# A gate loop before a mixture of experts: one small copy changes its queue, and the values are loaded a turn earlier into one more buffer

## The chip, the cores and the metric

The kernel runs on one core of one Trainium2 chip. The metric is the device time of one execution in microseconds (us); it is 389.04 us before the change, the median of three executions (388.29 to 390.93).

The core has five engines that run side by side, each through its own list of instructions in order: TensorE (PE in the profile; PEld are its weight loads), VectorE (DVE), ScalarE (ACT), GpSimd (POOL) and SyncE (SP). Transfers (DMAs) are issued by SP and by POOL here. Whoever issues a transfer first waits for what it depends on, and what stands behind it in the same list waits as well.

## The reference, cut to what matters

There are two parts. The first is a linear recurrence with a complex decay for each of 4 batches and 8 heads, over 768 steps with 48 channels; its output y is the input of the second part, a mixture of experts.

```python
def _attn_ref(q, k, v, a_re, a_im):
    mag = np.sqrt(a_re * a_re + a_im * a_im)
    scale = np.minimum(mag, 0.999) / (mag + 1e-06)
    a_re_n, a_im_n = (a_re * scale, a_im * scale)
    for t in range(S):
        new_re = ar * S_re - ai * S_im          # ar, ai: step t of a_re_n, a_im_n
        new_im = ar * S_im + ai * S_re
        kv = np.einsum('bhd,bhe->bhde', k[:, :, t], v[:, :, t])
        S_re, S_im = (new_re + kv, new_im)
        y[:, :, t] = np.einsum('bhd,bhde->bhe', q[:, :, t], S_re)

def _moe_ref(x, modality_id, w_gate, modality_bias, w1, w2):
    # each of the 3072 rows goes to the one expert (of 8) that its logits name:
    # out = gate weight * (relu(x @ w1[e]) @ w2[e])
```

All inputs and the output are float32.

## The kernel before

The steps are cut into 6 chunks of 128. A chunk of one batch is a unit of work; there are 24 units, in the order of chunk and then batch, and two units of the same chunk make a group. The products of decays inside a chunk become sums of logarithms and of angles, so the recurrence turns into masked matrix products inside a chunk and one state that goes from chunk to chunk. The state is multiplied by the moduli of the whole chunk, `mt`.

A turn `w` of the main loop takes a different stage of each of several units, so that all engines have work. This is the loop, cut to the calls that matter here:

```python
for w in range(-4, NU + 1):
    even = w % 2 == 0
    x = w // 2                      # group
    n = w + 1 if w < 0 else w       # unit
    unit(values, n + 2)             # SP: load V
    if even:
        phase(load_a, x + 6)        # SP: load a_re, a_im of a group (4 DMAs)
        phase(carries, x + 4)       # SP: load the angles carried over (cb)
        phase(decays2, x + 1)       # second half of mt
        phase(fractions, x + 3)
    else:
        phase(load_qk, x + 3)       # SP: load q, k of a group (4 DMAs)
        phase(decays, x + 2)        # SP: load mt
        hats(n + 3)
    unit(turned, n + 2)             # PE: transposes tKT, tQT
    ...
    unit(inner, n + 1)              # PE: wp, up; DVE: W, mid, U, state
    ...                             # even: sums and moduli of group x + 2
    unit(outer, n)                  # PE: yp
    ...
    unit(rows, n - 1)               # PE: xw; ACT: xr; POOL: x_rows
    ...
    if casts and (w > 9 or w % 3 == 1 and w > 0):
        cast = casts.pop(0)()       # POOL: 768 KB of expert weights to bf16, DRAM to DRAM
```

The scheduler may move a few calls of a turn against each other; the order of the calls is by and large the order in which a queue issues them.

V has four buffers of its own, used in turn. Elements 48 to 63 of each row stay zero:

```python
Vs = [un.tile([L, H, 64], F32, name=f"V{i}", bufs=1) for i in range(4)]
for V in Vs:
    nc.gpsimd.memset(V[:, :, D:64], 0.0)

def values(g, b):
    V = Vs[(g * B + b) % 4]
    nc.sync.dma_start(out=V[:, :, 0:D], in_=at(v, g, b))
```

Two products read V: `up` in the stage `inner` (line 300), which makes what the chunk adds to the state, and `yp` in the stage `outer` (line 322), a turn later. With that the buffer is free again.

The moduli go through DRAM, because they are needed with channels on partitions and are made with time on partitions. `moduli` writes the last row of `pm` to `m_scr` from POOL; `decays` reads it back as `mt` from SP, on 48 partitions; `decays2` copies `mt` to the next 48 partitions, because the real and the imaginary half of the state lie below each other:

```python
def moduli(x):
    ...
    nc.gpsimd.dma_start(out=m_scr[n0:n0 + NG]..., in_=pm[L - 1:L, 0]...)    # line 225

def decays(x):
    mt = un.tile([C, NG, H], F32, name="mt", bufs=4)
    nc.sync.dma_start(out=mt[0:D], in_=m_scr[n0:n0 + NG].rearrange("i h d -> d i h"))   # line 234

def decays2(x):
    mt = box["mt", x]
    nc.sync.dma_start(out=mt[D:C], in_=mt[0:D])                             # line 241
```

The copy of line 241 can be issued only when the load of line 234 has landed. DVE then uses both halves:

```python
nc.vector.tensor_tensor(new[:], U[:], box["mt", ...][...].broadcast_to([C, H, D]), Alu.mult)   # line 310
```

Other loads on the same SP queue are `ab` (a_re and a_im, two buffers), `qk` (q and k, two buffers), `cb`, and the writes of the gate weights `gw` into `x_rows`. Other transfers on the POOL queue are `f_scr` (angles), `m_scr`, `x_rows` (the rows y for the experts, from `xr`, two buffers) and the 16 weight casts. The second part, the experts, follows the loop and isn't touched by the change.

Of the kernel before, what the change touches and what calls it, by code (L numbers as in the profile page):

```python
# [11 lines left out]
F32 = mybir.dt.float32  # L12
# [11 lines left out]
def gate_loop(nc, ctx, tc, cpool, ident, q, k, v, a_re, a_im, sel, lg, x_rows, casts, make_router):  # L24
# [4 lines left out]
    B, H, S, D = q.shape  # L29
    L = 128  # L30
    G = S // L
    J = H // 2
    C = 2 * D
# [5 lines left out]
    un = ctx.enter_context(tc.tile_pool(name="un", bufs=2))  # L39
# [26 lines left out]
    def bank(shape, name):  # L66

        full = ps.tile([128, 512], F32, name=name, tag="bank", bufs=7)
        n = 1
        for s in shape[1:]:  # L70
            n *= s
        flat = full[0:shape[0], 0:n]
        if len(shape) == 2:
            return flat
        names = " ".join(f"x{i}" for i in range(len(shape) - 1))
        return flat.rearrange(f"p ({names}) -> p {names}", **{f"x{i}": s for i, s in enumerate(shape[1:])})


    Vs = [un.tile([L, H, 64], F32, name=f"V{i}", bufs=1) for i in range(4)]
    for V in Vs:  # L80
        nc.gpsimd.memset(V[:, :, D:64], 0.0)

# [8 lines left out]
    def table(name):  # L91
        then(nc.scalar.preload_act_table_set(name))  # L92
# [8 lines left out]
    def at(x, g, b):  # L101
        return x[b, :, g * L:(g + 1) * L, :].rearrange("h t d -> t h d")
# [134 lines left out]
    def decays2(x):  # L237

        if ("mt", x) in box:
            mt = box["mt", x]  # L240
            nc.sync.dma_start(out=mt[D:C], in_=mt[0:D])

    def both(x):
        return x[:, :, None, :].broadcast_to([L, H, 2, D])
# [1 line left out]
    def hats(w):  # L246

        if not 0 <= w < NU or (hats, w) in done:
            return
        done.add((hats, w))  # L250
        x, i = w // NG, w % NG
        cs = box["cs", x]
        pm = box["pm", x]
        qk = box["qk", x]
        qp = un.tile([L, H, D], F32, name="qp")
        nc.vector.tensor_tensor(qp[:], qk[:, 0, i], pm[:, 0, i], Alu.mult)
        kp = un.tile([L, H, D], F32, name="kp")
        nc.vector.tensor_tensor(kp[:], qk[:, 1, i], pm[:, 1, i], Alu.mult)
        Kh = un.tile([L, H, 2, D], F32, name="Kh", bufs=5)
        nc.vector.tensor_tensor(Kh[:], cs[:, i], both(kp[:]), Alu.mult)  # L260
        Qh = un.tile([L, H, 2, D], F32, name="Qh", bufs=3)
        nc.vector.tensor_tensor(Qh[:], cs[:, i], both(qp[:]), Alu.mult)
        box["hats", order[w]] = Qh, Kh

    def values(g, b):
        V = Vs[(g * B + b) % 4]
        nc.sync.dma_start(out=V[:, :, 0:D], in_=at(v, g, b))

    def turned(g, b):
# [14 lines left out]
    def inner(g, b):  # L284


        Kh, KT, QT = box.pop(("turned", g, b))
        V = Vs[(g * B + b) % 4]
        W = un.tile([L, H, L // 2], F32, name="W")
        wp = bank([L, H, L // 2], "wp")  # L290
        for h in range(H):
            for s in halves:
                nc.tensor.matmul(wp[s, h, :], KT[:, h, s], QT[:, h, s], start=True, stop=True)  # L293
        nc.vector.tensor_tensor(W[:], wp, mask2[:, None, :].broadcast_to([L, H, L // 2]), Alu.mult)
        old = state.get(b)
        more = g < G - 1
        ups = [bank([C, H, D], "up") for s in halves[:1 + more]]
        for h in range(H):
            for s, up in zip(halves, ups):
                nc.tensor.matmul(up[:, h, :], Kh[s, h].rearrange("t c d -> t (c d)"), V[s, h, 0:D], start=True, stop=True)  # L300
        mid = un.tile([C, H, D], F32, name="mid", bufs=3)
        if g:
            nc.vector.tensor_tensor(mid[:], old[:], ups[0], Alu.add)
        else:
            nc.vector.tensor_copy(mid[:], ups[0])
        if more:
            U = un.tile([C, H, D], F32, name="U")
            nc.vector.tensor_tensor(U[:], mid[:], ups[1], Alu.add)
            new = un.tile([C, H, D], F32, name=f"state{b}", bufs=2)
            nc.vector.tensor_tensor(new[:], U[:], box["mt", (g * B + b) // NG][:, b % NG, :, None].broadcast_to([C, H, D]), Alu.mult)  # L310
            state[b] = new
        box["inner", g, b] = QT, W, (old, mid)

    def outer(g, b):

        QT, W, states = box.pop(("inner", g, b))
        V = Vs[(g * B + b) % 4]
        yps = [bank([128, J, L // 2], "yp") for s in halves]
        for j in range(J):
            for u in range(2):  # L320
                for s, yp, S in zip(halves, yps, states):
                    nc.tensor.matmul(yp[u * 64:(u + 1) * 64, j, :], V[s, 2 * j + u, :], W[s, 2 * j + u, :], start=j == 0, stop=S is None and j == J - 1)  # L322
        yT = un.tile([128, J, L], F32, name="yT")
        for s, yp, S in zip(halves, yps, states):
            if S is not None:
                for j in range(J):
                    for u in range(2):
                        nc.tensor.matmul(yp[u * 64:u * 64 + D, j, :], S[:, 2 * j + u, :], QT[:, 2 * j + u, s], start=False, stop=j == J - 1)  # L328
            nc.scalar.copy(yT[:, :, s], yp)  # L329
        box["outer", g, b] = yT  # L330
# [22 lines left out]
    def phase(f, x):  # L353

        if 0 <= x < NX and (f, x) not in done:
            done.add((f, x))
            f(x)

    def unit(stage, w):
        if 0 <= w < NU and (stage, w) not in done:  # L360
            done.add((stage, w))
            stage(*order[w])
# [26 lines left out]
    for w in range(-4, NU + 1):  # L389


        even = w % 2 == 0
        x = w // 2

        n = w + 1 if w < 0 else w
        unit(values, n + 2)
        if even:
            phase(load_a, x + 6)
            phase(carries, x + 4)
            phase(decays2, x + 1)  # L400
            phase(fractions, x + 3)
        else:
            phase(load_qk, x + 3)
            phase(decays, x + 2)
            hats(n + 3)
            if w == -3:
                hats(0)
        unit(turned, n + 2)
        if even:
            if x + 2 < NX:  # L410
                table(EXP)
            if w < 0:
                phase(sums, x + 2)
                phase(moduli, x + 2)
            phase(logs, x + 4)
        elif x + 3 < NX:
            table(TRIG)
            phase(arctans, x + 4)
        unit(inner, n + 1)
        if even:  # L420
            phase(sums, x + 2)
            phase(moduli, x + 2)
            for f in late:
                f(act)
            late.clear()
        unit(outer, n)
        if even:
            hats(n + 3)
            phase(tangents, x + 4)
        else:  # L430
            phase(waves, x + 3)
            phase(squares, x + 5)
        unit(rows, n - 1)
        if not even:
            phase(angles, x + 4)
        if w == 0:
            rt = make_router(ctx, ps, bank)
        marks.append(chain[-1])
        if casts and (w > 9 or w % 3 == 1 and w > 0):
            cast = casts.pop(0)()  # L440
            tc.add_manual_dep(cast.ins, marks[-3].ins.name, mybir.DependencyInfo(mybir.DependencyClass.Sync, mybir.DependencyReason.DATA), reason="spreads the casts over the turns")
        open_ = [t for t in open_ if next(t, True) is None]
        if w - 1 in takes:
            open_.append(rt.take(takes[w - 1], w, late))
            next(open_[-1])
# [337 lines left out]
def kernel(  # L783
# [37 lines left out]
    with ExitStack() as gstack:  # L821
        rt = gate_loop(nc, gstack, tc, cpool, ident, q, k, v, a_re, a_im, sel, lg, x_rows, casts, lambda where, ps, bank: Router(nc, where, tc, cpool, ps, bank, lg, x_rows, moe_modality_id, moe_modality_bias, N, Dt, E, B, S // 128))
# [31 lines left out]
```

## Time and profile before

| | before |
|---|---|
| time, median of 3 | 389.04 us (388.29 to 390.93) |
| span of the profiled execution | 385.6 us |
| PE, DVE, ACT, POOL busy | 82%, 66%, 62%, 27% |
| first part (gate loop and router) | 0 to about 280 us of the span |
| experts | about 280 us to the end |
| V loads | 24, 192 KB each, median 4.0 us from issue to landing |
| `mt` load, `mt` copy | 10 each, 3 KB, median 3.5 and 2.4 us |
| weight casts | 16, 768 KB, median 8.4 and 8.7 us |

The page's first part gives the busy share of each engine over the whole span, its second the same in 40 slices of 9.6 us, with the clock that TensorE was granted and the share of the 16 DMA engines. Both stages have different limits, so the shares over the whole span say little; what matters is where in the slices the busiest engine of a stage has a hole, and which wait ended last there. That is in the list of waits, in the timeline of an engine, and in the chain of work that ended last.

### The profile page before, as it was taken

What the parts mean: (1) busy time and instruction counts of PE and PEld (TensorE: products, weight loads), DVE (VectorE), ACT (ScalarE), POOL (GpSimd) and SP (SyncE); (2) the same over time, 40 slices, a digit from 0 to 9 for tenths busy, and PEclk for the clock granted to TensorE, in tenths of its full rate; (3) what the DMA queues carried; (4) which work ended last, traced back from release to release, by engine and by line L of the source; (5) the groups of instructions that cost most, each with busy time, mean ns of one, the idle gap of its engine ahead of it and who ended that gap; (6) DMA issues with size and microseconds to landing.
All of it is one profiled execution on the core that took longest, in us unless ns stands there. A gap on an engine that the chain in (4) does not pass through costs nothing.

```text
span 385.6 us, 11163 instructions
## 1 busy us (share of the span) xinstructions
PE 317.4 (82%) x4533; PEld 259.5 (67%) x4533; DVE 256.3 (66%) x560; ACT 239.4 (62%) x410; POOL 105.2 (27%) x149
## 2 busy tenths in 40 slices
PE   0075799999999999990899999999219999999991
PEld 0033587787888878880778898998006777777780
DVE  2559989999988999947369899334803444444340
ACT  2869999999999997974359884343022323333331
POOL 6011102121120121211012213000074776767332
PEclk9998969999999999996599999999657999999998
DMA  9998878999988899999599998930199999999961
GB/s 143 187 161 166 174 115 155 182 190 172 196 158 166 178 161 183 151 200 167 91 190 165 188 188 150 201 65 23 31 393 363 415 403 405 411 406 406 414 256 41
DMA packets 164564, 81.04 MB, mean 210 GB/s; under 512 B 143807, under 2 KB 153332, under 8 KB 164514
## 3 DMA queue, kind: packets, MB, share of 16 engines
q1 hardware_dynamic: 147922, 57.94, 62.2%
q0 software_dynamic: 16592, 22.40, 27.7%
q8 instruction: 35, 0.57, 0.6%
q14 instruction: 15, 0.12, 0.1%
HBM read 85.71 MB, written 21.11 MB: 277 GB/s over the span
## 4 chain that ended last, share of the span: by engine, by line
PE 47%; ACT 14%; DMA 10%; issue 9%; DVE 6%; SPq 6%; POOL 5%; POOLq 1%; DVEq 0%; ACTq 0%
PE h_ps L740 7%; PE up L300 6%; PE y_ps L751 6%; PE wp L293 4%; PE xw L337 4%; PE yp L328 4%; DMA V<-in_v_dram 4%; ACT sq L95 3%; PE tKT L277 3%; PE tQT L277 3%; POOL out_dram L759 3%; SPq L109 3%; PE u L161 2%; PE yp L322 2%; PE ls L211 2%
## 5 line engine op out<-in xcount | busy, mean ns | idle before, releaser
L300 PE MATMUL up<-V,Kh 64*96 64x48 f32 x704 | 40.0, 253 | 11.4 <-DMA V<-in_v_dram 11.1
L744 ACT ACTIVATE hT<-h_ps 128x512 bf16<-128x512 f32 x31 | 18.5, 597 | 45.3 <-PE h_ps L740 45.3
L300 PEld LDWEIGHTS up<-V,Kh 64*96 64x96 f32 x704 | 36.7, 167 | 13.4 <-issue 11.2
L740 PE MATMUL h_ps<-xgT,w1t 128*128 128x256 bf16 (+1 forms) x456 | 45.7, 258 | 0.0
L751 PE MATMUL y_ps<-w2t,hT 128*128 128x384 bf16 x248 | 43.5, 326 | 0.2 <-DVE hT L742 0.2
L740 PEld LDWEIGHTS <-w1t 128*128 128x128 bf16 x456 | 38.9, 100 | 5.8
L161 PE MATMUL u<-tan,turn 128*128 128x384 f32 x48 | 23.3, 571 | 22.9 <-ACT tan L95 22.9
L759 POOL DMA_INDIRECT out_dram<-y_sb,idx x31 | 31.2, 1007 | 29.7 <-ACT y_sb L755 20.0
L717 POOL DMA_INDIRECT xg<-x_rows,idx x31 | 29.9, 965 | 34.0 <-ACT idx L701 25.1
L277 PE MATMUL tKT<-ident,Kh 128*96 128x128 f32 x192 | 26.9, 285 | 8.0 <-DVE Kh L260 8.0
L751 PEld LDWEIGHTS <-hT 128*128 128x128 bf16 x248 | 23.4, 98 | 14.1 <-DVE hT L742 0.3
L92 ACT ACT_TABLE_LOAD x25 | 32.1, 1283 | 1.2 <-PEq L838 0.8
L742 DVE TENSOR_SCALAR hT<-h_ps 128x512 bf16<-128x512 f32 x31 | 21.4, 691 | 16.7 <-PE h_ps L740 11.6
L277 PEld LDWEIGHTS tKT<-ident,Kh 128*96 128x96 f32 x192 | 22.4, 133 | 11.2 <-DVE Kh L260 5.3
L329 ACT COPY yT<-yp 128x256 f32<-128x256 f32 x48 | 16.8, 376 | 19.9 <-PE yp L328 19.7
L293 PE MATMUL wp<-QT,KT 96*64 96x64 f32 x768 | 28.5, 229 | 0.0
L293 PEld LDWEIGHTS wp<-QT,KT 96*64 96x64 f32 x768 | 25.1, 141 | 4.6 <-issue 2.1
L161 PEld LDWEIGHTS u<-tan,turn 128*128 128x128 f32 x48 | 9.5, 224 | 27.5 <-issue 25.6
L337 PE MATMUL xw<-sel,yT 128*128 128x104 f32 x192 | 28.0, 291 | 0.0
L278 ACT COPY KT<-tKT 96x512 f32<-96x512 f32 x48 | 26.0, 594 | 2.3 <-PE tKT L277 2.2
L278 ACT COPY QT<-tQT 96x512 f32<-96x512 f32 x48 | 26.4, 609 | 0.5 <-PE tQT L277 0.5
L344 POOL DMA_DIRECT2D x_rows<-xr x20 | 12.4, 621 | 52.0 <-ACT xr L340 51.9
(144 smaller groups left out, 674.6 us busy)
## 6 DMA issues: line engine op xcount, KB each, us to landing
w1t<-w1b SPq DMA_DIRECT2D x19, 768.0 KB, 11.6
w2t<-w2b SPq DMA_DIRECT2D x19, 768.0 KB, 12.5
w1b<-in_moe_w_dram POOLq DMA_DIRECT2D x8, 768.0 KB, 8.4
w2b<-in_moe_w_dram POOLq DMA_DIRECT2D x8, 768.0 KB, 8.7
ab<-in_a_re_dram SPq DMA_DIRECT2D x24, 192.0 KB, 4.6
ab<-in_a_im_dram SPq DMA_DIRECT2D x24, 192.0 KB, 4.7
qk<-in_q_dram SPq DMA_DIRECT2D x24, 192.0 KB, 4.6
qk<-in_k_dram SPq DMA_DIRECT2D x24, 192.0 KB, 4.7
```

The costliest lines, as they stand in the source:

```text
L92: then(nc.scalar.preload_act_table_set(name))
L161: nc.tensor.matmul(u, turn[:], tan[:, i], start=True, stop=False)
L277: nc.tensor.transpose(tp[:, i, :], src[:, h4 + i].rearrange("t c d -> t (c d)"), ident[:])
L278: nc.scalar.copy(T[name][:, h4:h4 + 4], tp)
L293: nc.tensor.matmul(wp[s, h, :], KT[:, h, s], QT[:, h, s], start=True, stop=True)
L300: nc.tensor.matmul(up[:, h, :], Kh[s, h].rearrange("t c d -> t (c d)"), V[s, h, 0:D], start=True, stop=True)
L337: nc.tensor.matmul(xw[:, j, :], yT[:, j, :], sel[:, j, :], start=True, stop=True)
L717: nc.gpsimd.indirect_dma_start(out=xg[:], out_offset=None, in_=x_rows, in_offset=bass.IndirectOffsetOnAxis(ap=idx[:, s, 0:1], axis=0))
L740: nc.tensor.matmul(h_ps[:, f, :], w1t[:, k, ff * 128:(ff + 1) * 128], xgT[:, k, :], start=(k == 0), stop=(k == KD - 1))
L742: nc.vector.tensor_relu(hT[:, g * nf:(g + 1) * nf], h_ps[:])
L751: nc.tensor.matmul(y_ps[:], hT[:, f, s * 128:(s + 1) * 128], w2t[:, f, :], start=(f == 0), stop=(f == NF - 1))
L759: sc = nc.gpsimd.indirect_dma_start(out=out, out_offset=bass.IndirectOffsetOnAxis(ap=idx[:, s, 1:2], axis=0), in_=y_sb[:], in_offset=None, ...
```

## The change

Two things are changed, both in what SP has to issue in the gate loop. The copy of `mt` is issued from POOL, so that SP doesn't stand at it until the load of `mt` has landed. And V is loaded one turn further ahead: at turn n the load of unit n + 3 instead of n + 2, for which there is a fifth buffer. (The old call stays in the loop; every unit is loaded once, so it acts only where the new call hasn't come before it.)

```diff
-    Vs = [un.tile([L, H, 64], F32, name=f"V{i}", bufs=1) for i in range(4)]
+    Vs = [un.tile([L, H, 64], F32, name=f"V{i}", bufs=1) for i in range(5)]
@@ decays2
-            nc.sync.dma_start(out=mt[D:C], in_=mt[0:D])
+            nc.gpsimd.dma_start(out=mt[D:C], in_=mt[0:D])
@@ values, inner, outer (the same edit in each)
-        V = Vs[(g * B + b) % 4]
+        V = Vs[(g * B + b) % 5]
@@ main loop
         unit(values, n + 2)
+        unit(values, n + 3)
         if even:
```

The arithmetic and the bytes moved are the same.

More of the change, by code (lines that the diff above doesn't have):

```diff
@@ L287, in inner @@
         Kh, KT, QT = box.pop(("turned", g, b))
-        V = Vs[(g * B + b) % 4]
+        V = Vs[(g * B + b) % 5]
         W = un.tile([L, H, L // 2], F32, name="W")
@@ L316, in outer @@
         QT, W, states = box.pop(("inner", g, b))
-        V = Vs[(g * B + b) % 4]
+        V = Vs[(g * B + b) % 5]
         yps = [bank([128, J, L // 2], "yp") for s in halves]
```

## The prediction

> **What bounds the kernel now.** I read the page's 40 slices first. PE is at 8 or 9 tenths through the gate loop, except in slices 18 and 19 (173 to 193 us), where it drops to 2 tenths and its granted clock halves. The later dip, slices 27 to 29, is the router's end and isn't touched.
>
> ```profile
> PE   0075799999999999990899999999219999999991
> ...
> PEclk9998969999999999996599999999657999999998
> DMA  9998878999988899999599998930199999999961
> ```
>
> The list of waits, longest first, says what ended it: one single wait of PE for a load of V. Beside it DVE waited 6.7 us for a load of `ab` in the same stretch.
>
> ```profile
> PE up L300 <- DMA V<-in_v_dram: 11.1, 1, 11.1
> ...
> DVE tan L125 <- DMA ab<-in_a_im_dram: 7.6, 3, 6.7
> ```
>
> The table by stretches of 8.7 us (one turn) has after each stretch PE, weight loads, DVE, ACT, POOL, then granted clock, DMA share, GB/s. PE does nothing in 175.5 to 184.2 and then runs at clock 0.50. DMA is full in the hole (1.08), but had slack before it (0.63) and after it (0.53).
>
> ```profile
> 149.40:158.10 8.70, 8.67 (x201) 8.01 (x202) 8.47 (x28) 8.70 (x17) 1.99 (x3) 1.00 0.63 130
> ...
> 175.50:184.20 8.70, 0.00 (x0) 0.00 (x0) 6.75 (x12) 4.55 (x7) 0.57 (x1) 0.61 1.08 161
> 184.20:192.90 8.70, 8.01 (x105) 7.55 (x106) 3.88 (x7) 3.08 (x5) 0.00 (x0) 0.50 0.53 92
> ```
>
> What it costs: in PE's timeline the same step, the first transposes of a turn, starts at 170.77 and next at 195.03. That is 24.26 us for one turn; the chain has its neighbours at 195.19, 204.05 and 212.76, so 8.7 to 8.9 us a turn. The hole costs about 15.5 us: 11.1 of waiting, and 4.4 because the work from 184.90 to 195.03 (10.1 us) takes 5.8 two turns earlier, from 155.75 to 161.51.
>
> ```profile
> 170.77 1.04 PE L277 MATMUL tKT<-ident,Kh 128*96 128x128 f32 x8
> ...
> 195.03 1.04 PE L277 MATMUL tKT<-ident,Kh 128*96 128x128 f32 x8
> ```
>
> Why were V and `ab` late? SP's own waits lead with the line that the change moves, and SP's timeline shows where it hurt: the load of `mt` is issued at 146.18, its copy at 154.48, and everything behind the copy stands for 7.6 us. Four `ab` loads end at 170.51 (+4.5 us to landing = 175.0, when DVE resumed). The V load of turn 14 is issued at 174.09, 0.3 us after PE had finished the `wp` products before it, and lands at 184.8.
>
> ```profile
> SPq L241 <- DMA mt<-m_scr: 29.0, 10, 7.6
> ```
>
> ```profile
> 146.18 0.62 SPq L234 DMA_DIRECT2D mt<-m_scr  x1
> 154.48 0.51 SPq L241 DMA_DIRECT2D mt<-mt  x1
> 155.09 0.54 SPq L267 DMA_DIRECT2D V<-in_v_dram  x1
> ...
> 164.94 5.53 SPq L109 DMA_DIRECT2D ab<-in_a_re_dram  x1
> 170.51 1.12 SPq L110 DMA_DIRECT2D ab<-in_a_im_dram  x1
> ...
> 174.09 0.38 SPq L267 DMA_DIRECT2D V<-in_v_dram  x1
> 174.56 10.54 SPq L576 DMA_DIRECT2D x_rows<-gw  x8
> ```
>
> Why did 192 KB take 10.7 us, against a median of 4.0? Because POOL issued a weight cast (768 KB) at 173.57. The queues' shares while the cast of 162.82 ran show it: q0 (POOL's) holds the engines, q1 (SP's loads) has 5.5%.
>
> ```profile
> q0 software_dynamic: 255, 0.52, 101.3%
> q1 hardware_dynamic: 117, 0.02, 5.5%
> ```
>
> **What the Trainium skill says.** (1) "DMA: Bandwidth & Descriptors", section "Queues, rings and completion order": a DMA engine takes turns between its queues packet by packet. The lines above agree: 255 packets of 2 KB against 117 of mostly 192 bytes, so the small ones get next to no bytes. A load issued within about 8 us of a cast is late. (2) Same page, "Two DMAs through the same engine are not ordered": who reads what an earlier DMA wrote must wait for its semaphore on the issuing engine. So line 241 stands in SP until `mt` has landed; the trace agrees, 29.0 us in 10 waits. (3) Same page, "Issuing engines are not separate DMA queues": another issuer brings no more bandwidth, only issue time. I agree as to bandwidth; the trace's gain is not the 0.51 us of issuing but the 7.6 us of standing. (4) "TensorE: Matmul & The Clock Gate", "What's actually happening": after an idle window of about 3.4 us the clock halves. The trace agrees: 0.50 after a hole of 11.1 us.
>
> **The change, part by part.** *Copy to POOL.* Ten copies of 3 KB leave SP; with them go up to 29.0 us of standing and 10 × 0.5 us of issuing, nearly all hidden today. On the path is the 7.6 us before 154.48. The built program keeps each queue's order, and SP's transfers each wait for the eighth before it. If all after 146.8 moves up by 7.6, the last `ab` lands at 175.0 − 7.6 = 167.4. *V a turn earlier.* Load n+3 at turn n into the fifth buffer waits for the same release as load n+2 did with four (turn n−2 done), so it adds no wait. In the new order V of turn 14 stands ahead of the three q/k loads and four `ab` loads instead of behind them: issued at about 147, not 174. The load of turn 15 takes its old place and isn't needed before 182. One more 192 KB ahead of `ab` costs about 1 us (from 192 to 195 us, with no cast running, SP's loads moved 210 GB/s), so `ab` at about 168.4; DVE wanted it at 168.5. From there DVE needs 5.9 us to reach W (175.15 to 181.10 today), so W ends at about 175.1, and PE, done with `up` at 173.7 + 1.5 = 175.2, goes on. *Added:* one memset of 0.2 us on POOL at the start (hidden), and the wait for `mt`, now in POOL. POOL is 27% busy, but its casts, `x_rows` and `f_scr` now queue behind that wait. At the bad place I put `mt` landing at about 166 and the cast, ready at 162.8, 4 us late. The state needs this copy at about 177, and the `xr` two turns on reuses the buffer of an `x_rows` that then lands at about 175.5, and is due at about 178: both in time, with 2 to 8 us to spare. *Sum:* −15.5 us for the hole; +2 us, a guess, for what of these margins doesn't hold. That is −13.5 us, 389.0 to 375.5.
>
> **The rivals.** *A: the ab wait takes the place of the V wait.* If the wait for `mt` only changes queue and `ab` still lands at 175, W ends at 181.8 and PE resumes there instead of at 187.6. Gain 5.8, 383. For it: DVE's 6.7 us wait is real and lies under PE's. Against it: SP stood idle for 7.6 us just before, with DMA at 0.63. *B: POOL becomes the blocker.* A copy that queues behind a cast lands some 8 us later (`x_rows` has a median of 7.7 us, the copy on SP 2.4). If the state waits for it in every pair of turns, 10 × 1 to 2 us come back: 385 to 395. Against it: today the copies are issued 10 us or more before DVE reads them in seven of ten cases. *C: DMA has no room.* From 132 to 254 us its share is about 1.0; 15 us less would need 1.15. Against it: the stretches with 0.63 and 0.53 are 7 us of room, stretches of 1.2 occur, and after 254 us the share is 0.12 with 13 us of PE work to go, so the last casts can end later. If it bound all the same, 380 to 382. *D: nothing of this is on the path*, because the slowest run's hole is an accident of timing: the three times of 388.3 to 390.9 lie too close for that.
>
> **Range and chances.** 373.5 would be the whole hole. Nothing else in the loop is waiting for SP (PE is at 8.70 of 8.70 in most turns), so below 371 is unlikely. A and C end near 382, B higher. Range 371 to 383. The line for faster by 2% is 381.3: 0.82 for faster, 0.14 within, 0.04 slower.
>
> **What would show it.** Right: no wait of PE for V; slices 18 and 19 of PE at 9 and clock 1.00 throughout the loop; SP's waits without line 241 and a POOL wait for `mt` in its place; `ab` landing before DVE asks. Wrong in the `ab` step: DVE's wait for `ab` stays at 5 us or more and PE's hole is shorter but there. Wrong in the POOL step: DVE line 310 or ACT line 340 waits for DMA. The prediction as a whole fails if a new wait of PE over 3.4 us appears, since that brings the half clock back as well.

## The result and the profile after

The changed kernel takes 374.28 us in the median of 4 executions (372.81 to 377.14), the kernel before 388.67 us beside it (386.02 to 390.93): a ratio of 0.964, 95% interval 0.956 to 0.973. 375.5 was predicted. A second measurement on another chip gave 374.27 us (5 executions) against 388.3, a ratio of 0.970 (0.963 to 0.977).

On the page of the changed kernel, whose slices are 9.4 us, the hole of PE is gone, and the clock stays at 9 from slice 7 to slice 26; the dip after it, slices 27 to 30, is the router's end. Slices 5 and 6, counted from 0 as before, have clock 5 and 7; the last section is about that.

```profile
PE   0065879899999999999999999995159999999991
...
PEclk9998957999999999999999999998558999999998
DMA  9998885999989989997999999801599999999950
```

In the table by stretches (columns as before), the two stretches that held the hole and the half clock now have PE busy without a break at clock 1.00, with a DMA share of 1.11 and 1.13 (1.08 and 0.53 before).

```profile
175.50:184.20 8.70, 8.70 (x164) 7.50 (x162) 8.56 (x16) 8.67 (x15) 2.10 (x4) 1.00 1.11 180
184.20:192.90 8.70, 8.70 (x160) 7.28 (x158) 6.82 (x12) 7.80 (x16) 0.89 (x2) 1.00 1.13 214
```

In PE's timeline the first transposes of the turn, which took 24.26 us from one turn to the next, now take 8.72.

```profile
173.46 1.04 PE L277 MATMUL tKT<-ident,Kh 128*96 128x128 f32 x8
...
182.18 1.04 PE L277 MATMUL tKT<-ident,Kh 128*96 128x128 f32 x8
```

The waits: line 241 is no longer among SP's. GpSimd stands there instead, much longer than SP did (84.0 us against 29.0). PE doesn't wait for V at all, DVE has no wait for `ab` inside the loop, and ACT's wait for `x_rows` has grown from 1.7 to 4.4 us.

```profile
POOL mt L241 <- DMA mt<-m_scr: 84.0, 10, 14.3
...
ACT xr L340 <- DMA x_rows<-xr: 4.4, 2, 2.6
```

SP's timeline shows what that bought. The `mt` load that stood at 146.18 is issued at 139.69, V of unit 14 (the prediction calls it V of turn 14) at 141.20 (it was 174.09), the last of the four `ab` loads at 155.98 (170.51). The V load in the old place, 164.32, is that of unit 15. GpSimd's timeline shows the price: the copy that follows the `mt` load of 170.67 goes out at 173.34, after 13.4 us of standing, and the cast that was issued at 162.82 before only behind it.

```profile
139.69 0.33 SPq L234 DMA_DIRECT2D mt<-m_scr  x1
141.20 0.38 SPq L267 DMA_DIRECT2D V<-in_v_dram  x1
...
155.98 2.98 SPq L110 DMA_DIRECT2D ab<-in_a_im_dram  x1
...
164.32 0.57 SPq L267 DMA_DIRECT2D V<-in_v_dram  x1
```

```profile
173.34 0.52 POOL L241 DMA_DIRECT2D mt<-mt  x1 [13.36 <-DMA mt<-m_scr]
173.90 0.73 POOL L462 DMA_DIRECT2D w1b<-in_moe_w_dram  x1
```

The casts are as greedy as they were. While one runs (178 to 181 us), SP's queue has a tenth of the engines:

```profile
q0 software_dynamic: 378, 0.60, 100.7%
q1 hardware_dynamic: 211, 0.04, 9.7%
```

### The profile page after: what moved, and what is told of

It is laid out like the page before. It is cut to its first block, busy times and chain, and to the rows that moved or that the text cites. A ratio compares the mean times of both kernels' runs of the same rounds, so it can differ in the third digit from the quotient of the medians.

```text
span 375.2 us, 11166 instructions
## 1 busy us (share of the span) xinstructions
PE 317.1 (85%) x4533; PEld 258.7 (69%) x4533; DVE 256.3 (68%) x560; ACT 239.0 (64%) x410; POOL 110.8 (30%) x160
## 4 chain that ended last, share of the span: by engine, by line
PE 48%; ACT 18%; issue 10%; DMA 9%; POOL 5%; DVE 5%; SPq 3%; POOLq 1%; ACTq 0%; DVEq 0%
PE h_ps L741 7%; PE up L300 6%; PE y_ps L752 6%; PE wp L293 5%; ACT sq L95 4%; PE yp L328 4%; PE xw L337 3%; PE tKT L277 3%; PE tQT L277 3%; POOL out_dram L760 3%; PE ls L211 3%; DMA x_rows<-xr 3%; ACT L92 2%; PE yp L322 2%; DMA ab<-in_a_im_dram 2%
## 5 line engine op out<-in xcount | busy, mean ns | idle before, releaser
L741 PE MATMUL h_ps<-xgT,w1t 128*128 128x256 bf16 (+1 forms) x456 | 46.5, 261 | 0.0
L241 POOL DMA_DIRECT2D mt<-mt x10 | 5.4, 535 | 84.0 <-DMA mt<-m_scr 84.0
L337 PE MATMUL xw<-sel,yT 128*128 128x104 f32 x192 | 27.1, 285 | 0.0
L758 DVE TENSOR_SCALAR y_sb<-y_ps,xg 128x384 f32<-128x384 f32 x12 | 7.4, 618 | 28.6 <-PE y_ps L752 26.0
L277 PE MATMUL tQT<-ident,Qh 128*96 128x128 f32 x192 | 26.6, 284 | 0.0
```

The source lines that it names most:

```text
L277: nc.tensor.transpose(tp[:, i, :], src[:, h4 + i].rearrange("t c d -> t (c d)"), ident[:])
L337: nc.tensor.matmul(xw[:, j, :], yT[:, j, :], sel[:, j, :], start=True, stop=True)
L741: nc.tensor.matmul(h_ps[:, f, :], w1t[:, k, ff * 128:(ff + 1) * 128], xgT[:, k, :], start=(k == 0), stop=(k == KD - 1))
```

## The experiments

**How they are compared.** Ratios are against the kernel before on the same chip. To see the gate loop alone, I read off each trace when `up` (line 300) starts in unit 4 and in unit 23, 19 turns later. The difference leaves out the loop's start and the experts. The kernel before needs 260.92 − 82.56 = 178.36 us, the changed one 248.93 − 85.78 = 163.15 us.

| kernel | 19 turns, us | longest turns, us | ratio, 95% interval |
|---|---|---|---|
| before | 178.36 | 20.5, 13.0 | |
| the whole change, first and second measurement | 163.15, 163.53 | 9.8, 9.9 | 0.964 (0.956–0.973), 0.970 (0.963–0.977) |
| copy only, twice | 163.23, 162.36 | 9.8, 9.8 | 0.977 (0.972–0.981), 0.973 (0.968–0.977) |
| look ahead only | 183.40 | 18.8, 17.1 | 1.012 (1.003–1.020) |
| casts moved | 181.42 | 20.1, 11.6 | 1.026 (1.021–1.031) |
| two loads, look ahead | 170.04 | 15.2, 9.8 | 0.997 (0.990–1.004) |
| GpSimd stands, SP too | 183.29 | 13.9, 12.8 | 1.006 (0.995–1.017) |
| two loads, GpSimd stands | 170.01 | 14.5, 10.5 | 0.981 (0.974–0.988) |
| two loads, old look ahead | 169.59 | 12.7, 12.2 | 0.983 (0.975–0.991) |
| copy later on SP | 181.37 | 16.7, 13.4 | 0.991 (0.987–0.995) |
| casts not in the loop | 162.35 | 9.8, 9.7 | |
| whole change, third `xr` | 162.29 | 9.8, 9.7 | 0.965 (0.961–0.969) |

The profiled executions of "look ahead only", "GpSimd stands, SP too" and "copy later" lie over 1.5% above the fastest of their kernel, so their 19 turns are at the long end; the ratios leave such executions out. The first four experiments ran on a chip where the kernel before took 404.4 us; its gate loop isn't slower (copy only: 163.23 there, 162.36 elsewhere).

**Copy only.** The kernel before with line 241 on GpSimd; V keeps four buffers.

```diff
-            nc.sync.dma_start(out=mt[D:C], in_=mt[0:D])
+            nc.gpsimd.dma_start(out=mt[D:C], in_=mt[0:D])
```

> The kernel before with one part of the change: the copy of mt is issued from POOL, V keeps four buffers and its old lookahead. Theory (SP's standing at the copy made both V and ab late): V of turn 14 is issued about 7 us earlier, at about 167, and the cast that would starve it now waits in POOL for mt, so PE's wait for V is under 2 us, DVE's wait for ab under 2 us, and the time is 373 to 378. Rival (the lookahead of V is what counts): V still comes at the moment it is needed, PE waits 3 to 8 us and the half clock comes back, 380 to 387.

Measured: 0.977, and the 19 turns of the whole change (163.23 against 163.15), without a wait of PE for V. SP's timeline shows why V needs no second turn of lead: freed, SP issues the same V load, in its old place, at 157.96 instead of 174.09, ahead of the cast (170.32).

```profile
156.10 1.76 SPq L172 DMA_DIRECT2D cb<-f_scr  x1
157.96 0.42 SPq L267 DMA_DIRECT2D V<-in_v_dram  x1
```

**Look ahead only.** The changed kernel with line 241 back on SP.

```diff
-            nc.gpsimd.dma_start(out=mt[D:C], in_=mt[0:D])
+            nc.sync.dma_start(out=mt[D:C], in_=mt[0:D])
```

> The kernel after with the copy of mt back on SP: fifth buffer and lookahead only. Theory (two waits lie over each other, V's in PE and ab's in DVE): V comes in time, but ab still lands at about 175 and DVE waits 5 us or more for it, PE then waits for W; about 383 (380 to 386). Rival (the V wait alone made the hole): no hole, 373 to 377.

Measured: 1.012 (1.003 to 1.020), resting on two executions of this kernel: no gain, and perhaps a loss. At the old place the theory's step can be read in the trace (174 to 194 us). V comes in time, PE begins `up` of unit 14 at 173.63, but `ab` is still late: DVE waits 6.9 us for it, until 175.32, ACT waits for DVE, and PE for ACT. PE stops for 4.8 us after two products and does the other 30 in 2.79 us at a granted clock of 0.50, so that 18.8 us pass from unit 14 to unit 15. So the two waits did lie over each other, and the look ahead takes away only V's.

```profile
PE up L300 <- ACT xr L340: 4.8, 1, 4.8
...
DVE tan L125 <- DMA ab<-in_a_im_dram: 6.9, 1, 6.9
DVE state L310 <- DMA mt<-mt: 4.6, 1, 4.6
```

The state then waits 4.6 us for the copy of `mt`, which holds PE up for 0.9 us. A second hole follows that the theory didn't have: in the turn of 17.1 us the chain has a k load that takes 15.73 us, across a cast issued at 207.67 and one at 214.88, before DVE's line 258 can go on.

```profile
210.01 15.73 DMA qk<-in_k_dram
...
225.84 0.56 DVE kp L258
```

**Casts moved.** The kernel before with other turns for the casts.

```diff
-        if casts and (w > 9 or w % 3 == 1 and w > 0):
+        if casts and w in (1, 2, 4, 5, 7, 10, *range(14, 25)):
```

> The kernel before, SP's list of transfers unchanged; only the weight casts move: none in turns 11 to 13, two of them early at turns 2 and 5, one each turn from 14 on. Theory (a cast starves SP's small packets, and that alone makes the mt load take 8.3 us and the V load 10.7 us): between turns 11 and 14 the mt load lands in 2 to 4 us, no wait of PE for V there, 374 to 379 if no new hole opens later. Rival (SP's order and its waits are enough for the hole, the casts don't matter): the hole stays, 387 to 390.

Measured: 1.026. The old hole is gone and another stands 60 us earlier: `ab` takes 9.36 us at 108.80, the cast having been issued at 109.10, and unit 8 follows unit 7 after 20.1 us. With the casts in these two places, another load is late each time, and some turn has a hole.

```profile
108.80 9.36 DMA ab<-in_a_im_dram
...
118.29 0.96 DVE tan L125
```

**Two loads.** The changed kernel with the copy replaced by a second load from DRAM on SP. SP never stands at a copy, GpSimd neither.

```diff
             nc.sync.dma_start(out=mt[0:D], in_=m_scr[...].rearrange("i h d -> d i h"))
+            nc.sync.dma_start(out=mt[D:C], in_=m_scr[...].rearrange("i h d -> d i h"))
@@ decays2
-            nc.gpsimd.dma_start(out=mt[D:C], in_=mt[0:D])
```

> The kernel after without the copy: the second half of mt is a second load from DRAM on SP, right behind the first, so neither SP nor POOL waits for mt to land. Theory (POOL's 84 us of waiting for mt is off the path; what gain there was is had already): same as after within 1.5 us, 373 to 376. Rival 1 (POOL's waiting holds back casts, x_rows and f_scr and costs time through ACT's wait for x_rows): 369 to 372. Rival 2 (ten more loads of 768 packets of 4 bytes on SP take DMA time from V, ab, q and k): 377 to 382.

Measured: 0.997, with one hole before unit 19. The chain shows the second half of `mt` landing 10.51 us after its issue at 210.73, with a cast issued at 210.82.

```profile
210.73 10.51 DMA mt<-m_scr
...
221.36 0.55 DVE state L310
```

This is where my first explanation wavered: SP was free in this run, too, and yet little was won. I formed another: GpSimd, standing at the copy, holds the casts back, and that is what counts. The next three runs put that to the test.

**GpSimd stands, SP too.** The kernel before, with a tiny operation of GpSimd (some 0.8 us each) where the copy would stand. It reads the first half of `mt` and so waits for the load.

```diff
+            gate = un.tile([D, 1], F32, name="gate", bufs=2)
+            nc.gpsimd.tensor_scalar(gate[:], mt[0:D, 0, 0:1], 1.0, None, Alu.mult)
             nc.sync.dma_start(out=mt[D:C], in_=mt[0:D])
```

> The kernel before, its copy left on SP, so that SP stands as before; GpSimd gets one tiny operation at the place of the program where the copy of the first experiment stood, which reads the loaded half of mt. GpSimd therefore stands there until the load of mt has landed, and the casts, x_rows and f_scr behind it are held back in the same way, but SP is not freed. Theory now (the standing of GpSimd holds the casts back until SP's loads ahead of mt have landed, and this is what removes the hole): 0.97 to 0.985 of the kernel before, no wait of PE for V over 3.4 us. First theory (freeing SP is what counts): 0.995 to 1.005, the hole stays.

Measured: 1.006 (0.995 to 1.017). GpSimd stood as meant (107.7 us in ten waits), and SP still stood at the copy, if less (18.7 us). The old hole is not there in this profile: PE waits 0.3 us for V of unit 14. But nothing is won in the whole: `x_rows`, held back with the casts, now stopped ACT for 11.8 us and through it PE, and near the end PE waited 3.8 us for a V. So holding the casts back can move this hole, but, with SP standing, it isn't what makes the kernel faster, and the new theory falls.

```profile
POOL gate L242 <- DMA mt<-m_scr: 107.7, 10, 19.5
...
ACT xr L342 <- DMA x_rows<-xr: 11.8, 4, 4.5
```

**Two loads, GpSimd stands.** The second load on SP as above, and the tiny operation; four buffers and the old look ahead.

```diff
+            nc.sync.dma_start(out=mt[D:C], in_=m_scr[...].rearrange("i h d -> d i h"))
@@ decays2
-            nc.sync.dma_start(out=mt[D:C], in_=mt[0:D])
+            gate = un.tile([D, 1], F32, name="gate", bufs=2)
+            nc.gpsimd.tensor_scalar(gate[:], mt[0:D, 0, 0:1], 1.0, None, Alu.mult)
```

> The kernel before with four buffers and the old look ahead; the second half of mt is a second load from DRAM on SP, so that SP never stands at a copy, and GpSimd has the tiny operation that reads the loaded first half and stands for it. Both queues are as in the copy-only experiment, but no copy is issued by GpSimd. Theory now: as the copy alone, 0.97 to 0.985. If freeing SP and standing of GpSimd each give a part: also 0.97 to 0.985; if neither matters and it was the copy's own place: 1.00.

Measured: 0.981, and a turn of 14.5 us before unit 20. There ACT waits 5.2 us for an `x_rows`:

```profile
210.08 9.65 DMA x_rows<-xr
...
219.83 0.49 ACT xr L342
```

**Two loads, old look ahead.** The same without the tiny operation: SP free, GpSimd free.

```diff
+            nc.sync.dma_start(out=mt[D:C], in_=m_scr[...].rearrange("i h d -> d i h"))
@@ decays2
-            nc.sync.dma_start(out=mt[D:C], in_=mt[0:D])
```

> The same two loads on SP without the tiny operation: SP free, GpSimd free, four buffers and the old look ahead. First theory (freeing SP counts): 0.97 to 0.985 as the copy alone. Theory now (GpSimd must stand): 0.99 to 1.02, with a hole of PE over 3.4 us somewhere in the gate loop, as in the run with two loads and the look ahead (0.997).

Measured: 0.983. So freeing SP gives more than half of the gain in the loop without GpSimd standing at all (169.59 against 178.36, where the whole change has 163.15). What is missing to 163 lies in two turns of 12.2 and 12.7 us: the second half of `mt`, issued 0.6 us after a cast, lands after 7.69 us, the state waits for it, and PE then works on at half clock (32 products `up` in 2.73 us; 1.49 at full clock).

```profile
172.87 7.69 DMA mt<-m_scr
...
180.68 0.16 DVE state L310
```

The 19 turns are the same with the look ahead (170.04) as without it. The two ratios of this pair, 0.997 and 0.983, were taken on different chips. In the two profiles 4.1 us of the difference is the start of the loop (unit 4 begins at 85.83 and at 81.76 us); the rest wasn't tried.

**The whole change on a second chip.**

> The changed kernel itself, on the chip of the experiments. The copy alone gave 0.977 here and the look ahead alone 1.012. If the look ahead adds nothing: 0.972 to 0.985, and the last product up at the same time as with the copy alone, give or take the 3 us of the clock window. If it adds something beside the copy: 0.965 or less, as the 0.964 of the first measurement.

Measured: 0.970 (0.963 to 0.977), 374.27 us, loop 163.53, as the first time. The ratio lies between the two ranges expected, so it doesn't decide on the look ahead.

**Copy later on SP.** The kernel before; the copy stays on SP but is put behind the next four `ab` and the next q and k loads.

```diff
             copy = nc.sync.dma_start(out=mt[D:C], in_=mt[0:D])
+            if ("qload", x + 2) in box and x > 1:   # order only: after the third of those q/k loads
+                tc.add_manual_dep(copy.ins, box["qload", x + 2].ins.name, ...NoSync...)
@@ main loop: the call of decays2 moves from the even turn to the odd one after it, behind load_qk
```

> The kernel before with the copy of mt left on SP, but later in SP's order: behind the next four loads of ab and the next q and k loads instead of right behind the load of mt. By then mt has landed, so SP should hardly stand (under 1 us at the copy), GpSimd doesn't stand either, no packet is added, V keeps four buffers and the old look ahead. First theory (SP's standing is what cost the time): 0.96 to 0.98, no wait of PE for V, the last product up near 246 us. Rival (the copy has to leave SP, or GpSimd has to stand): 0.99 to 1.01 with a hole of 7 us or more. A risk of its own: the copy comes too late for the state, seen as a wait of DVE line 310.

Measured: 0.991 (0.987 to 0.995), with a spread of 380.8 to 397.3 us. The median of all 21 executions, 387.5 us, is that of the kernel before, 387.8 us, so a gain is seen in the better executions alone. SP's standing is gone, but the risk named there came true: issued behind everything else, the 3 KB copy meets a cast. This one takes until 227.90, and DVE stands for 7 us. (The profile writes "issue" there, because the wait sits in a semaphore instruction ahead of the product.)

```profile
215.50 0.90 SPq L241 DMA_DIRECT2D mt<-mt  x1
```

```profile
220.38 0.55 DVE L310 TENSOR_TENSOR U<-mid,up 96x384 f32<-96x384 f32 x1
...
227.98 0.56 DVE L312 TENSOR_TENSOR state<-U,mt 96x384 f32<-96x384 f32 x1 [6.98 <-issue]
```

**Casts not in the loop.** The kernel before without casts among the turns. They were to follow the loop; the scheduler put them ahead of it instead, so the loop starts some 60 us late and the whole takes 432.8 us. Only the loop is to be read.

```diff
-        if casts and (w > 9 or w % 3 == 1 and w > 0):
+        if False:
@@ after the loop
+    while casts:
+        casts.pop(0)()
```

> The kernel before with all 16 weight casts issued after the gate loop instead of in it; the whole takes longer, only the gate loop is to be read. If the casts' packets are what makes SP's loads late (and the copy stands so long only for that): the mt copy stands SP for under 3 us each time, no wait of PE over 3.4 us from 60 us on, last product up at 246 us or before. If SP's standing costs by itself: the hole of 8 us or more stays and the last up is near 260.

Measured: 19 turns in 305.34 − 142.99 = 162.35 us, no hole, with the copy on SP, four buffers and the old look ahead. (The start of the last `up` can't be held against 246 us, since the loop began late.) SP's standing at the copy shrinks from 29.0 us to 10.5, the longest from 7.6 to 2.3:

```profile
SPq L241 <- DMA mt<-m_scr: 10.5, 8, 2.3
```

So the casts are the root. The stand at the copy is long because a cast is running when `mt` is loaded, and it hurts because the next cast then meets the load of V.

**Copy only, again**, and **the whole change with a third `xr` buffer**, on one chip.

```diff
-        xr = un.tile([L, J, C], BF16, name="xr")
+        xr = un.tile([L, J, C], BF16, name="xr", bufs=3)
```

> The copy alone once more, on another chip and beside a like number of runs. If the look ahead of V adds nothing, the ratio is that of the whole change (0.964 and 0.970 in two measurements), 0.962 to 0.974, some 374 us where the kernel before has 388; if the look ahead adds the rest, 0.975 to 0.985, 379 us or more.

> The changed kernel with a third buffer for xr, so that ACT needn't wait until GpSimd's late x_rows has landed. The trace of the changed kernel has ACT waiting for it 4.4 us in all, one turn 0.9 us long for it. If that wait is on the path: 1 to 2 us less than the changed kernel, 0.960 to 0.968, and ACT line 340 without a wait for DMA; if it is hidden: the same, 0.964 to 0.971.

Measured: copy only 375.25 us, 0.973 (0.968 to 0.977); with the third buffer 373.37 us, 0.965 (0.961 to 0.969), and no wait of ACT for `x_rows` in its list. The intervals of copy only and of the whole change overlap, the medians are 1 us apart, the loops of all four profiles lie between 162.4 and 163.5 us: no share of the look ahead can be shown. With the third buffer the turn of 9.6 us at unit 17 is gone (longest turns now 9.8, 9.7 and 9.5), but it is gone in the repeat of copy only as well, which has two `xr` buffers and waits of ACT for `x_rows` of 5.2 us: its loop is as short, 162.36 against 162.29 us. The median with the third buffer is the lowest of all, 0.9 us under the changed kernel's, which is too little to call it faster.

## Why the prediction was right, point by point

- **The hole costs 15.5 us.** Right: 178.36 − 163.15 = 15.2 us.
- **All of SP moves up by 7.6 us.** Right in kind, too small: the last `ab` load moved by 170.51 − 155.98 = 14.5 us. I moved SP by the one stand ahead of the hole; earlier stands fall away, too (the `mt` load is itself 146.18 − 139.69 = 6.5 us earlier).
- **V a turn earlier takes it out of the cast's way.** It does (141.20, predicted about 147), but it wasn't needed: with the copy alone V goes out at 157.96 and the loop is as short. I gave a share of the cure to a part that has none that can be shown. Alone it gained nothing (1.012), because `ab` stayed late (6.9 us) and a k load came late in another turn.
- **The cast of 162.82 is 4 us late on GpSimd.** Too small: it was issued at 173.90, 11 us later. I had `mt` landing at 166; its load was issued only at 170.67. It cost little, as the small margins held: ACT waits 4.4 us for `x_rows` in two places, DVE never for `mt`. That ACT's waits cost anything in the loop isn't shown: it is as short with 5.2 us of them (162.36) as with none (162.29).
- **+2 us, a guess.** The medians differ by 14.4 us, 1.1 less than the hole. In the spans of the profiled executions, 385.6 and 375.2 us, it adds up as −15.2 in the 19 turns, +3.2 in the loop's start and +1.6 behind the last `up` (from the first read of the experts' rows to the end 105.7 us before, 107.4 after). The guess stood for margins in the loop, and nothing was lost there; that the sum comes within 1.2 us of the measured time is luck in that part.
- **Packets by turns.** The reading that the lines agree with this is loose: with strict turns SP's queue would have had a packet for each of the cast's as long as it had work, but the lines have 117 against 255 and 211 against 378. What the runs show are the shares, 5.5% and 9.7%.
- **Rival A** (`ab` takes over) fell: no wait of DVE for `ab` in the loop. Its step is real, though: with the look ahead alone it is what happened. **Rival B** (GpSimd blocks) didn't happen here, but it is real: where GpSimd stands without SP being freed, `x_rows` comes late and nothing is gained (1.006). **Rival C** (no room) fell: both stretches run at a share of 1.1. **Rival D** (an accident) is half true: which turn gets the hole hangs on the timing of the casts, but in every profile of a kernel that has the copy on SP right behind the load and the casts in the loop (four here) some turn gets one.

**What the runs show together.** With SP freed by a second load, four buffers and the old look ahead, the ratio is 0.98 twice (0.983, and 0.981 with GpSimd standing), though no copy is on GpSimd; holding GpSimd back alone gives nothing (1.006). Two more runs with SP freed won little: two loads with the look ahead 0.997, the late copy 0.991. What these four lack of the whole gain lies, as far as it was traced, in turns in which `mt` or `x_rows` itself comes late: as a second load, or as a late copy, `mt` runs into a cast and the state waits. On GpSimd the copy stands directly ahead of the cast in one list (173.34 and 173.90), so it is on its way when the cast begins. The 20 landings of it that the traces of four runs give (the whole change twice, once with a third `xr`, and copy only again) took 2.6 to 5.6 us, the seven of the late copy 2.5 to 12.4 us.

The loads of V, `ab`, q and k in the gate loop show the same, counting those for which the trace gives a landing. Issued within 8 us after a cast, they took 4.3 to 12.8 us in the kernel before (12 loads) and 7.7 to 10.6 us in the changed one (9); issued up to 5 us ahead of a cast, with none in the 8 us before, 2.8 to 5.1 us (12) and 2.8 to 5.5 us (15). That this order protects `mt` on GpSimd fits all runs, but was argued from these times, not tried alone.

## What to carry to other kernels

Look for the small transfer at which a busy queue stands, and ask which large one made it slow: the wait on PE's list was for V, the cause was a cast on another queue. When a dependent small transfer is moved, ask two things: what stands behind it in its new list, and does it go out before the large one or after. The second is argued here from the times of landing. And test the parts of a change one by one; here the part that names PE's wait (V earlier) did nothing that can be shown, and the other alone gave as short a loop as both.

## What the runs showed of the hardware

**One and the same turn took 9 or 12 us, by the clock granted.** In the turn of unit 1, the same instructions took 9.05 us at clock 0.99 in the kernel before and 12.24 us at 0.71 in the changed one (the columns of the table by stretches, kernel before first):

```profile
54.22:63.27 9.05, 9.05 (x142) 7.13 (x141) 7.35 (x14) 8.30 (x13) 0.73 (x1) 0.99 0.70 87
```

```profile
54.25:66.49 12.24, 12.24 (x142) 9.57 (x141) 7.35 (x14) 8.41 (x13) 1.12 (x2) 0.71 0.63 87
```

It isn't the change's doing: copy only had the short turn in one run (63.19 − 54.23 = 9.0 us) and the long one in the other (66.53 − 54.27 = 12.3), and so had the changed kernel (12.2 and 9.0). What decides it isn't shown. One profile can be 3 us better or worse for this alone.

**A load of 3 KB can have nearly as many packets as one of 192 KB.** `mt` gathers 48 × 16 = 768 single numbers; between 146 and 156 us, while it is loaded, the trace of the kernel before holds 834 packets of 4 bytes. V has 128 × 8 = 1024 rows of 192 bytes. In time the small ones weigh less, 9 ns in the median against 15 ns in this loop, but the second load of `mt` was no small thing to add. Whether that is what cost the runs with two loads wasn't tried.
